# Softmax denominators on a Trainium2 core: which key tiles are added together by DMA, by an elementwise engine and by TensorE

## The chip, the cores and the metric

The kernel runs on one core of one Trainium2 chip. The metric is the device time of one execution in microseconds (us), and lower is better. The kernel before takes 4543.79 us, the median of 3 runs (4541.69 to 4547.17).

The engines are called by the profile's names: PE is TensorE (matmul; PEld is its weight load), DVE is VectorE, ACT is ScalarE, POOL is GpSimd and SP is SyncE, which here only issues DMAs. A name ending in q is an engine's sequencer.

## The reference

The program runs the same two-layer stack twice: an attention layer A and a routed feed-forward layer B, each with a residual. The change touches only the attention of A, which runs twice. Cut to that:

```python
qkv = (x @ wqkv).reshape(B, S, 3, H, Dh).transpose(2, 0, 3, 1, 4)   # S = 2048, H = 32 heads, Dh = 32
q, k, v = qkv[0], qkv[1], qkv[2]
scores = jnp.einsum("bhqd,bhkd->bhqk", q, k) * Dh ** -0.5
p = _softmax(scores, axis=-1)
o = jnp.einsum("bhqk,bhkd->bhqd", p, v)
return o.transpose(0, 2, 1, 3).reshape(B, S, D) @ wo
```

A softmax needs, for every head and query, the sum of the exponentials over all 2048 keys. The kernel leaves the product with v unnormalised and divides by that sum later, so the sums are a piece of work of their own. The change is about how these sums are made.

## The kernel before, in words

**Units and steps.** The attention of a layer is cut into NU = 32 units. A unit is a group of 4 heads with 512 queries. Each unit walks over NT = 16 key tiles of 128 keys, one tile in one step, so a layer has NS = 512 steps. Step s belongs to unit u = s // 16 and key tile kt = s % 16.

**What a step does.** The order of the instructions on every engine is the order in which the Python code emits them. In an ordinary step the loop at L1148 emits: `pre_mm` (matmuls L706 with their row maxima, DVE L714, for the queries of a unit 25 steps ahead), two half steps (`half_step`: scores by PE at L721 into a `pre` PSUM tile, then the exponential by ACT at L1112, two heads at a time), `pre_mm` again, then `pv_step(s - 1)` (PE L1043, the product of the tile before with v), and last `rest_of_step(s)`. The exponentials of a step fill one tile `P[s]`, 128 keys by 4 heads by 512 queries, float32, 1 MB. In the code below P1 means the tile of key tile 1 of its unit.

**Buffers for P.** `P` has PB = 9 buffers. A new tile takes a buffer in the order in which the program gave them back. A buffer is given back by the last instruction that uses its tile, and the exponential that fills it anew waits until this instruction is done.

**The sums.** The 16 tiles of a unit are added up over the keys in three ways:

- A *merge* (`merge`, L1056) is a DMA issued by POOL that adds one P tile to another in place: `merge(u, a, b)` makes P[a] += P[b]. It must wait until PE has read P[a] for the product with v.
- An *add* (`acc_add`, L1053) is one elementwise instruction over 128 x 2048 numbers that adds a P tile to the accumulator `acc` of the unit. It runs on POOL, or on DVE where its last argument is true. The first add of a unit takes two P tiles.
- A *direct* tile goes into the final sum on PE as it is. `sum_mm` (L1063) multiplies a matrix of ones with each direct tile and with `acc`, four matmuls (one for each head) for each of them, into one PSUM tile `st`. ACT copies the result to `sm` (L1073), and SP stores it.

**The order of this work.** `unit_events(left)` lists, for a unit that has `left` units after it, at which step each of these is emitted: (step, "mid" or "end" of `rest_of_step`, priority, what, arguments). A step of 16 or more lies in the next unit. `emit` collects what is due at a step from the unit before and from this one, sorts it and issues it. `EVENTS` holds three lists: for the last unit (`left` 0, all adds on DVE), for the last but one (`left` 1) and for all others. POOL works its list strictly in order, so an instruction that waits holds up all behind it.

**Before**, an ordinary unit has 5 merges (P0+=P1, P6+=P7, P8+=P9, P10+=P11, P12+=P13, emitted at steps 2, 8, 11, 13, 15), 8 adds on POOL (P2 and P3 first, then P0, P5, P4, P6, P8, P10, P12), and the direct tiles 14 and 15. The sum is emitted at step 22, which is step 6 of the next unit. In the last unit but one the adds from step 9 on are on DVE.

**The maxima on SP's queue.** The row maxima of the next unit are put together by DVE in step 6 (`nm_combine`) and step 7 (`nm_row`). SP writes them to DRAM (`nmx<-nmr`, four DMAs) and reads them back into a row of the query tile (`q<-nmx`, two DMAs). The scores of the next unit need them. All of SP's DMAs stand in one queue in the order of the code: the four stores of a sum (`sd<-sm`), then these, and one load of queries, keys or values in each step (`loads`).

**The end of a layer.** `pre_mm` runs 25 steps ahead, so from step 487 there is none. From step 488 (`threes`, L1146) three steps are emitted together, and a third score tile takes the PSUM of two `st` tiles. In step 487 there is no `pv_step`.

Of the kernel before, what the change touches and what calls it, by code (L numbers as in the profile page):

```python
# [19 lines left out]
NT = S // 128  # L20
# [3 lines left out]
NU = NG * QC  # L24
# [9 lines left out]
PB = 9  # L34


MERGED = ((2, 0), (8, 6), (11, 8), (13, 10), (15, 12))
ADDED = ((5, 3), (6, 0), (9, 5), (12, 4), (14, 6), (15, 8), (16, 10), (20, 12))
FIRST = 2
DIRECT = (14, 15)  # L40
LAST_DIRECT = (13, 14, 15)


SLOT_ROWS = (64, 33)
SUM_AT = 22

KEYS_AT = {(2, 14 + 3 * i): slice(i * 512, i * 512 + 512) for i in range(3)}
KEYS_AT[3, 3] = slice(3 * 512, S)

ON_DVE = 9


def unit_events(left):

    if left == 0:
        return [(k + 1, "mid", 1, "add", (k, 0 if k == 1 else None, True)) for k in range(1, NT) if k not in LAST_DIRECT]
    ev = [(at, "end", 0, "merge", (k, k + 1)) for at, k in MERGED]
    ev += [(at, "end", 1, "add", (k, FIRST if at == ADDED[0][0] else None, left == 1 and at >= ON_DVE)) for at, k in ADDED]  # L60
    return ev + [(SUM_AT, "mid", 5, "sum", ())]


EVENTS = [unit_events(i) for i in range(3)]


@with_exitstack
def tile_kernel(ctx, tc, x, wqkv, wo, w_r, w_gate, w_up, w_down, out):
# [29 lines left out]
    def ps_st():  # L98
        return banks["now"][1].tile([128, 512], F32, name="st", bufs=1 if banks["wide"] else 3)

    def ps_pre():
        return psum.tile([128, 1024], F32, name="pre", bufs=2)

    def ps_pv():
        return psum.tile([128, 512], F32, name="pv")
# [544 lines left out]
    def layer(n, src, dst, prev=None, following=None):  # L650
# [93 lines left out]
        with ExitStack() as pst:  # L744
# [209 lines left out]
            for k, (c, wb, i) in enumerate(steps):  # L954
# [26 lines left out]
                at = b - (1, 8)[c == 0]  # L981
# [31 lines left out]
        with sbuf(f"at{n}", bufs=2) as aw:  # L1013
            KS[1] = aw.tile([128, 2, 2, S], F32R, name="ks1", bufs=1)
            P, PV, ACC = {}, {}, {}
# [41 lines left out]

            def sum_mm(u):
                p = ps_st()
                parts = [P[u * NT + k] for k in (DIRECT if u < NU - 1 else LAST_DIRECT)] + [ACC.pop(u).rearrange("p (h c) -> p h c", h=4)]  # L1060
                for i, a in enumerate(parts):
                    for h in range(4):
                        pe.matmul(p[32 * h:32 * h + 32, :], ones32, a[:, h, :], start=(i == 0),  # L1063
                                  stop=(i == len(parts) - 1), tile_position=(0, 32 * h))
                return p
# [12 lines left out]
            def sum_out(u):  # L1078
                store_sum(u, sum_mm(u), aw.tile([128, 512], F32, name="sm", bufs=1))
# [13 lines left out]
            def emit(s, where):  # L1093
                u, kt = divmod(s, NT)
                todo = []
                for back in (1, 0):
                    v = u - back
                    if 0 <= v < NU:
                        todo += [(kt + NT * back, pri, fn, args, v) for (k, pos, pri, fn, args) in EVENTS[min(NU - 1 - v, 2)]
                                 if k == kt + NT * back and pos == where]  # L1100
                for k, _, fn, args, v in sorted(todo, key=lambda e: (-e[0], e[1])):
                    fns[fn](v, *args)

            for i in range(4):
# [11 lines left out]
            def rest_of_step(s):  # L1116
                u, kt = divmod(s, NT)
                pr = pre_rows[s + LEAD] if s + LEAD < NS else None
                emit(s, "mid")
                if pr and pr[1] == 15:  # L1120
                    nm_combine(pr[0])
                if (s + LEAD) % NT == 0 and NT <= s + LEAD - NT < NS:
                    nm_row((s + LEAD) // NT - 1)
                emit(s, "end")
                if s == NS + 1:
                    shared["sum"] = sum_mm(NU - 1)
                if s == NS - 20:
                    shared["first"] = aw.tile([128, 512], F32, name="sm", bufs=1)[:, 0:256]
                    sum_load(shared["first"], 0)
                if s == NS - 17:  # L1130
                    recip(shared["first"], 0)
                if s < NS and kt == 0:
                    queue_loads(u)
                    if u == NU - QC:
                        loads.extend((load_wo, a) for a in range(KD))
                if s == (NU - QC) * NT + 1:
                    right.close()
                    shared["wor"] = ExitStack()
                    wop = shared["wor"].enter_context(sbuf(f"wor{n}", side="right"))
                    shared["WOR"] = wop.tile([128, KD, D], F32, name="wor", bufs=1)  # L1140
                if loads:
                    f, *args = loads.pop(0)
                    f(*args)
# [42 lines left out]
        if True:  # L1186
# [81 lines left out]
            for t in range(NT - 2 if n else NT):  # L1268
                oh, ol = OT.pop(t)
                p = ps_pre()  # L1270
# [60 lines left out]
        if n:  # L1331

            parts = ffn.first_rows(rcols)
            waste = ps_pre()
            p = [[waste[:, h] for h in halves], [ps_st(), ps_pv()]]
            (ah, al), (bh, bl) = (OT.pop(t) for t in (NT - 2, NT - 1))
            both = range(2)
            todo = [(i, x, wol, a, both) for i, x in ((0, ah), (1, bh)) for a in range(KD)]
# [99 lines left out]
```

## Time and profile before

| what | us |
|---|---|
| median of 3 runs | 4543.79 |
| lowest and highest run | 4541.69, 4547.17 |
| the profiled execution | 4545.36 |
| its span, first to last instruction | 4543.6 |
| PE busy | 4497.7 (99%) |
| POOL busy | 3169.1 (70%) |
| DVE busy | 3156.8 (69%) |
| ACT busy | 2426.5 (53%) |

The profile shows one execution. It gives the busy time of each engine, the chain of work that ended last, groups of equal instructions with mean durations and with the idle time ahead of them, and a timeline. The attention runs from about 570 to 2030 us and again in the second layer; between the first and the last units it is strictly periodic, so one unit can be read for all. A shape such as 128x2048 is partitions by elements. Each matmul of the code appears as two records in the trace (8192 records on L1043 for 4096 calls). "x8" in a timeline row means 8 such records in a row.

### The profile page before, as it was taken

What the parts mean: (1) busy time and instruction counts of PE and PEld (TensorE: products, weight loads), DVE (VectorE), ACT (ScalarE), POOL (GpSimd) and SP (SyncE); (2) the same over time, 40 slices, a digit from 0 to 9 for tenths busy, and PEclk for the clock granted to TensorE, in tenths of its full rate; (3) what the DMA queues carried; (4) which work ended last, traced back from release to release, by engine and by line L of the source; (5) the groups of instructions that cost most, each with busy time, mean ns of one, the idle gap of its engine ahead of it and who ended that gap; (6) DMA issues with size and microseconds to landing.
All of it is one profiled execution on the core that took longest, in us unless ns stands there. A gap on an engine that the chain in (4) does not pass through costs nothing.

```text
span 4543.6 us, 73545 instructions
## 1 busy us (share of the span) xinstructions
PE 4497.7 (99%) x29241; PEld 2686.0 (59%) x29241; DVE 3156.8 (69%) x4975; ACT 2426.5 (53%) x2574; POOL 3169.1 (70%) x1239
## 2 busy tenths in 40 slices
PE   9999999999999999999999999999999999999998
PEld 7888755555555555548877786554555555555583
DVE  2211588888888888886522225888888888888763
ACT  3322266767676767670222222776767676767600
POOL 4444378989888889835633343898989898889252
PEclk9999999999999999999999999999999999999998
DMA  6757477777777768759698774777768677777598
GB/s 206 209 174 204 135 170 152 174 153 164 162 167 155 173 143 180 169 131 241 183 319 276 253 208 126 168 161 161 170 144 183 148 166 161 167 155 180 145 275 327
DMA packets 329719, 833.62 MB, mean 183 GB/s; under 512 B 43996, under 2 KB 160732, under 8 KB 280206
## 3 DMA queue, kind: packets, MB, share of 16 engines
q1 hardware_dynamic: 275454, 476.43, 35.8%
q0 software_dynamic: 45248, 325.67, 35.4%
q10 hardware_dynamic: 8672, 26.81, 2.3%
q8 instruction: 230, 3.77, 0.3%
q14 instruction: 115, 0.94, 0.1%
HBM read 384.34 MB, written 119.47 MB: 111 GB/s over the span
## 4 chain that ended last, share of the span: by engine, by line
PE 94%; DMA 2%; DVE 2%; issue 1%; POOL 1%; ACT 0%; SPq 0%; ACTq 0%; POOLq 0%; DVEq 0%
PE pv L1043 22%; PE pre L721 21%; PE st L839 17%; PE st L706 16%; PE pre L839 5%; PE pre L1283 5%; PE st L1063 4%; PE pv L549 1%; PE pre L706 1%; PE pv L839 0%; DMA ord<-rd 0%; PE pre L808 0%; DMA wraw<-in_A_wqkv_dram 0%; DVE acc L1053 0%; PE third L721 0%
## 5 line engine op out<-in xcount | busy, mean ns | idle before, releaser
L714 DVE TENSOR_REDUCE nm<-st 128x1 f32<-128x512 f32 x3916 | 2433.6, 684 | 374.7 <-PE st L706 368.8
L1112 ACT ACTIVATE P<-pre 128x1024 f32<-128x1024 f32 x2016 | 1955.2, 1022 | 704.2 <-PE pre L721 515.6
L1053 POOL TENSOR_TENSOR acc<-acc,P 128x2048 f32<-128x2048 f32 x422 | 2038.4, 4830 | 84.3 <-DMA P<-P 74.7
L721 PE MATMUL pre<-q,ks 64*128 64x512 f32 (+1 forms) x8064 | 1117.8, 395 | 1.7 <-ACT P L1112 1.7
L1043 PE MATMUL pv<-P,v 128*32 128x512 f32 x8192 | 1088.4, 605 | 4.5 <-DMA v<-vd 4.5
L706 PEld LDWEIGHTS st<-ks,q 64*128 64x128 f32 x3916 | 546.5, 184 | 906.8 <-DVE nm L714 765.3
L706 PE MATMUL st<-ks,q 64*128 64x512 f32 x3916 | 982.8, 470 | 0.4
L721 PEld LDWEIGHTS pre<-q,ks 64*128 64x128 f32 (+1 forms) x8064 | 765.2, 186 | 162.1 <-ACT P L1112 27.0
L1056 POOL DMA_DIRECT2D P<-P x310 | 294.2, 949 | 279.2 <-PE st L706 184.6
L854 DVE TENSOR_TENSOR lo<-st,hi 128x512 fp32r<-128x512 f32 x128 | 88.4, 691 | 528.0 <-ACT hi L853 507.9
L774 POOL TENSOR_TENSOR ohl<-wraw,ord 128x2048 fp32r<-128x2048 f32 (+1 forms) x54 | 222.5, 4124 | 308.4 <-ACT ord L769 292.7
L774 POOL TENSOR_TENSOR wl<-wraw,wh 128x2048 fp32r<-128x2048 f32 (+1 forms) x54 | 222.6, 4126 | 303.3 <-ACT wh L773 284.4
L853 ACT CAST hi<-st 128x512 fp32r<-128x512 f32 x128 | 75.4, 589 | 490.9 <-PE st L839 488.6
L1043 PEld LDWEIGHTS pv<-P,v 128*32 128x32 f32 x8192 | 163.3, 108 | 265.4 <-issue 258.2
L1053 POOL TENSOR_TENSOR acc<-P 128x2048 f32<-128x2048 f32 x62 | 295.2, 4761 | 11.0 <-ACT P L1112 11.0
L1283 PE MATMUL pre<-woh,ohl 128*128 128x512 f32 x960 | 223.4, 390 | 1.7 <-DVE pre L1316 0.9
L168 POOL TENSOR_TENSOR rs<-mv,eps_c 128x1 f32<-128x1 f32 x64 | 29.2, 456 | 264.7 <-DVE mv L166 264.7
L1283 PEld LDWEIGHTS pre<-woh,ohl 128*128 128x128 f32 x960 | 179.6, 188 | 42.1 <-ACT ohl L1214 2.1
L839 PE MATMUL st<-xh,wh 128*128 128x512 f32 x512 | 201.2, 393 | 0.0
L839 PE MATMUL st<-xh,wl 128*128 128x512 f32 x512 | 199.3, 389 | 0.0
L839 PE MATMUL st<-xl,wh 128*128 128x512 f32 x512 | 199.2, 389 | 0.0
L1214 ACT CAST ohl<-ord 128x1024 fp32r<-128x1024 f32 x32 | 33.6, 1051 | 272.1 <-DVE ord L1205 81.7
(389 smaller groups left out, 4069.0 us busy)
## 6 DMA issues: line engine op xcount, KB each, us to landing
P<-P POOLq DMA_DIRECT2D x310, 1024.0 KB, 8.9
wraw<-in_A_wqkv_dram SPq DMA_DIRECT2D x96, 1024.0 KB
q<-qh SPq DMA_DIRECT2D x256, 128.0 KB
ks<-kh SPq DMA_DIRECT2D x112, 256.0 KB
fw<-in_B_w_down_dram SPq DMA_DIRECT2D x17, 1024.0 KB
vd<-vn SPq DMA_DIRECT2D x32, 512.0 KB
qh<-hi SPq DMA_DIRECT2D x64, 256.0 KB
ql<-lo SPq DMA_DIRECT2D x64, 256.0 KB
```

Source lines behind the costliest of these rows:

```text
L706: pe.matmul(ps[b], Q[u][rows, i, 0, qt * 128:(qt + 1) * 128], KS[(u // QC) % 2][rows, i, 0, j * 512:(j + 1) * 512], start=True, stop=True, ...
L714: dve.tensor_reduce(NM[u][:, j, 2 * i + b:2 * i + b + 1, qt], ps[b], axis=AX.X, op=OP.max, negate=True)
L721: pe.matmul(p[:, b * 512:(b + 1) * 512], KS[(u // QC) % 2][rows, i, slot, kt * 128:(kt + 1) * 128], Q[u][rows, i, slot, :], start=(slot == ...
L774: pool.tensor_tensor(wl[:, sl], raw[:, sl], wh[:, sl].bitcast(F32), op=OP.subtract)
L839: pe.matmul(p, *pair(a, l, r), start=(a == 0 and k == 0), stop=(a == KD - 1 and k == 2))
L854: dve.tensor_tensor(lo, p, hi.bitcast(F32), op=OP.subtract)
L1043: pe.matmul(PV[u][32 * h:32 * h + 32, :], V[g][:, kt, 32 * h:32 * h + 32], P[s][:, h, :], start=(kt == 0), stop=(kt == NT - 1), tile_posit ...
L1053: (dve if on_dve else pool).tensor_tensor(o, a, P[u * NT + k].rearrange("p h c -> p (h c)"), op=OP.add)
L1056: pool.dma_start(P[u * NT + a], P[u * NT + b], accum_op=OP.add)
L1063: pe.matmul(p[32 * h:32 * h + 32, :], ones32, a[:, h, :], start=(i == 0), stop=(i == len(parts) - 1), tile_position=(0, 32 * h))
L1112: act.activation(P[s][:, 2 * i:2 * i + 2, :].rearrange("p h c -> p (h c)"), p, AF.Exp, scale=SCALE)
L1283: pe.matmul(p[:, bl], l[:, a, :], r[a][:, bl], start=(k == 0 and a == 0), stop=(k == 2 and a == KD - 1))
```

## The change

The two lists of steps become `SUMS` (ordinary units) and `BEHIND_SUMS` (the last unit but one). Ordinary units get six merges instead of five. One of them adds a tile to its predecessor, as all did before (P4+=P5); the other five add a tile to its successor (P2+=P1, P8+=P7, P10+=P9, P13+=P12, P15+=P14). Adds on POOL remain eight. Tile 15 alone is direct, and it then holds tile 14 too. The last unit but one gets three merges instead of five, ten adds on DVE instead of six, and one direct tile. The last unit is as before. The sum of a unit is emitted one step later (23 instead of 22). `emit` sorts by priority first and by age second, where it was the other way round; a step ending in .5 has the priority of 0.5, behind a whole one of the same step.

```diff
-MERGED = ((2, 0), (8, 6), (11, 8), (13, 10), (15, 12))
-ADDED = ((5, 3), (6, 0), (9, 5), (12, 4), (14, 6), (15, 8), (16, 10), (20, 12))
-FIRST = 2
-DIRECT = (14, 15)
+SUMS = (
+    (3, "merge", 2, 1), (5, "merge", 4, 5), (6, "add", 0, 3), (7, "add", 6), (9, "merge", 8, 7), (10, "add", 2), (11, "merge", 10, 9),
+    (11.5, "add", 4), (12, "add", 11), (14, "merge", 13, 12), (14.5, "add", 8), (16, "merge", 15, 14), (17, "add", 10), (19.5, "add", 13))
+DIRECT = (15,)
+
+BEHIND_SUMS = (
+    (3, "merge", 2, 1), (5, "merge", 4, 5), (6, "add", 0, 3), (7, "vadd", 6), (8, "vadd", 2), (9.5, "vadd", 9), (10, "merge", 8, 7), (11, "vadd", 4),
+    (11.5, "vadd", 10), (12, "vadd", 11), (13, "vadd", 12), (14, "vadd", 8), (15, "vadd", 13), (16, "vadd", 14))
+BEHIND_DIRECT = (15,)
 LAST_DIRECT = (13, 14, 15)
...
-SUM_AT = 22
+SUM_AT = 23
...
-ON_DVE = 9
...
-    ev = [(at, "end", 0, "merge", (k, k + 1)) for at, k in MERGED]
-    ev += [(at, "end", 1, "add", (k, FIRST if at == ADDED[0][0] else None, left == 1 and at >= ON_DVE)) for at, k in ADDED]
+    ev = []
+    for at, what, k, *other in (SUMS, BEHIND_SUMS)[left == 1]:
+        args = (k, *other) if what == "merge" else (k, *(other or [None]), what == "vadd")
+        ev.append((int(at), "end", at % 1, "merge" if what == "merge" else "add", args))
     return ev + [(SUM_AT, "mid", 5, "sum", ())]
...
-                parts = [P[u * NT + k] for k in (DIRECT if u < NU - 1 else LAST_DIRECT)] + [ACC.pop(u).rearrange("p (h c) -> p h c", h=4)]
+                parts = [P[u * NT + k] for k in (LAST_DIRECT, BEHIND_DIRECT, DIRECT)[min(NU - 1 - u, 2)]] + [ACC.pop(u).rearrange("p (h c) -> p h c", h=4)]
...
-                for k, _, fn, args, v in sorted(todo, key=lambda e: (-e[0], e[1])):
+                for k, _, fn, args, v in sorted(todo, key=lambda e: (e[1], -e[0])):
```

In the order of POOL's queue an ordinary unit now reads: P2+=P1, (add P13 of the unit before), P4+=P5, add P0 and P3, add P6, P8+=P7, add P2, P10+=P9, add P4, add P11, P13+=P12, add P8, P15+=P14, add P10.

## The prediction

> **What bounds the kernel now.** I read the page first, then one attention unit in windows and in the timeline, engine by engine.
>
> ```profile
> PE 4497.7 (99%) x29241; PEld 2686.0 (59%) x29241; DVE 3156.8 (69%) x4975; ACT 2426.5 (53%) x2574; POOL 3169.1 (70%) x1239
> PE 94%; DMA 2%; DVE 2%; issue 1%; POOL 1%; ACT 0%; SPq 0%; ACTq 0%; POOLq 0%; DVEq 0%
> ...
> 1119.92:1165.72 45.80, 45.80 (x348) 23.17 (x344) 40.14 (x67) 32.12 (x35) 41.06 (x14) 1.00 0.72 153
> 1165.72:1211.52 45.80, 45.80 (x348) 23.18 (x344) 40.13 (x67) 32.09 (x35) 40.98 (x14) 1.00 0.79 175
> ```
>
> The chain that ended last is 94% PE. The windows are two units, cut at the period of the sums below: PE is busy for all 45.80 us of each, so a unit is bound by PE's own instructions. POOL is busy 41 of these, which looks like 5 us to spare, but its time counts in another way: a late add or merge keeps a P buffer, the exponential waits, then PE. The last two columns are the DMA engines' share and GB/s.
>
> ```profile
> 958.37 0.59 ACT L1073 COPY sm<-st 128x512 f32<-128x512 f32 x1 [2.40 <-PE st L1063]
> 1004.17 0.59 ACT L1073 COPY sm<-st 128x512 f32<-128x512 f32 x1 [2.40 <-PE st L1063]
> ...
> 1136.16 0.50 PE L706 MATMUL st<-ks,q 64*128 64x512 f32 x2
> ...
> 1138.74 1.90 PE L1063 MATMUL st<-P,ones 128*32 128x512 f32 x16
> 1140.46 1.04 PE L1063 MATMUL st<-acc,ones 128*32 128x512 f32 x8
> 1141.43 0.50 PE L706 MATMUL st<-ks,q 64*128 64x512 f32 x2
> ...
> 1144.13 0.50 PE L706 MATMUL st<-ks,q 64*128 64x512 f32 x2
> ```
>
> Two sums are 45.80 apart. A plain step is 1144.13 - 1141.43 = 2.70 us. The step with the sum took 1141.43 - 1136.16 = 5.27, so the sum of three tiles costs 2.57. Its two direct tiles run from 1138.74 to 1140.46: 0.86 each.
>
> **The change part by part.** *One direct tile less.* Each layer has 31 units with one direct tile fewer, 62 in all: 62 x 0.86 = 53.3 us of PE (0.85 to 0.87 each: 52.7 to 53.9). The new unit is 44.95 us. All of this is on the path, provided nothing else becomes late.
>
> *The sixth merge, on POOL.*
>
> ```profile
> 1144.78 0.88 POOL L1056 DMA_DIRECT2D P<-P  x1 [2.70 <-PE st L706]
> 1145.39 4.88 POOL L1053 TENSOR_TENSOR acc<-acc,P 128x2048 f32<-128x2048 f32 x1
> 1150.18 0.93 POOL L1056 DMA_DIRECT2D P<-P  x1
> ...
> 1161.00 1.01 POOL L1056 DMA_DIRECT2D P<-P  x1
> 1161.62 5.00 POOL L1053 TENSOR_TENSOR acc<-acc,P 128x2048 f32<-128x2048 f32 x1
> 1167.21 4.59 POOL L1053 TENSOR_TENSOR acc<-acc,P 128x2048 f32<-128x2048 f32 x1 [0.59 <-DMA P<-P]
> ...
> 1175.39 4.57 POOL L1053 TENSOR_TENSOR acc<-acc,P 128x2048 f32<-128x2048 f32 x1 [2.72 <-DMA P<-P]
> 1179.92 4.58 POOL L1053 TENSOR_TENSOR acc<-P 128x2048 f32<-128x2048 f32 x1
> 1184.58 4.57 POOL L1053 TENSOR_TENSOR acc<-acc,P 128x2048 f32<-128x2048 f32 x1
> ```
>
> A merge with the add behind it occupies POOL for 1150.18 - 1144.78 = 5.40 us, a plain add for 4.6 (1179.92 to 1184.58). Five pairs and three adds are 40.8 us; the new six and two are 41.6, of 44.95. There remain 3.3 us a unit, if the waits fit. For that a timetable is needed.
>
> ```profile
> 1006.73 0.50 PE L706 MATMUL st<-ks,q 64*128 64x512 f32 x2
> 1007.07 1.11 PE L721 MATMUL pre<-q,ks 64*128 64x512 f32 x8
> ...
> 1007.80 1.94 ACT L1112 ACTIVATE P<-pre 128x1024 f32<-128x1024 f32 x2 [0.78 <-PE pre L721]
> ...
> 1008.44 1.06 PE L1043 MATMUL pv<-P,v 128*32 128x512 f32 x8
> ```
>
> In a step the exponential runs from 1.07 to 3.01 us after the step begins, and the product of the previous tile ends at 2.77. I count from the start of a new unit: step 7 begins at 18.9, step 8, behind a sum of now 1.71, at 23.3, the next unit at 44.95. A merge into Pk goes out some 0.35 us after Pk's product, that is at the start of step k+2 plus 0.4. POOL's queue then runs: P2+=P1 at 11.2; add P13 of the unit before, to 16.65; P4+=P5 at 16.65; adds P0+P3 and P6, to 26.65; P8+=P7 at 29.15, after 2.5 idle; add P2; P10+=P9 at 34.6; adds P4, P11, to 44.6; P13+=P12 at 44.6; add P8; P15+=P14 at 50.0; add P10, to 55.4; and the next P2+=P1 at 56.15. It closes with 3.3 us idle. Buffers that an add gives back (by the order of the changed program) are asked for later: P13's, free at 16.65, by the exponential of step 7 at 20.0; that is the tightest. The others have 4 us or more. The sum wants P13 and P15 at 21.6.
>
> Buffers that a merge's source gives back wait for the landing of the DMA. The tightest are P12's, asked for in step 4 at 44.95 + 11.9 = 56.8, and P14's, in step 6 at 62.2. Both leave 12.2 us from issue to landing. About 0.5 more costs PE nothing: a second half of scores starts 0.5 us after its `pre` tile is normally free. All else has 13 us or more.
>
> ```profile
> L1056 POOL DMA_DIRECT2D P<-P x310: 850/918/1703, 577.8 to 4232.8; - x155
> DMA to landing us min/median/max: 6.9/8.9/14.6
> ...
> q0 software_dynamic: 641, 4.60, 50.7%
> q1 hardware_dynamic: 1398, 2.37, 21.0%
> ...
> 1135.00:1140.00 5.00, 5.00 (x42) 2.07 (x44) 4.22 (x8) 3.41 (x4) 4.22 (x2) 1.00 0.05 10
> 1140.00:1145.00 5.00, 5.00 (x44) 2.40 (x38) 2.94 (x6) 2.53 (x3) 2.30 (x2) 1.00 0.01 1
> 1150.00:1155.00 5.00, 5.00 (x42) 2.42 (x38) 4.71 (x8) 3.69 (x4) 5.00 (x3) 1.00 1.05 212
> 1160.00:1165.00 5.00, 5.00 (x40) 2.83 (x40) 4.57 (x9) 3.50 (x4) 5.00 (x3) 1.00 1.02 241
> ```
>
> Landings go from 6.9 to 14.6. In the first unit the merges' queue q0 took 50.7% of 45.80 = 23.2 us for 4.60 MB, 5.3 us for a merge. At a share of 0.72 to 0.79 a unit needs 33 to 36 us of the DMA engines; one merge more makes 38 to 41.5, of 44.95. It still fits, and there was room: the share was 0.05 and 0.01 from 1135 to 1145. The long landings of before are the last merges of four that go out 5.4 us apart (1144.78 to 1161.00) while key loads run: the one of 1161.00 landed at 1175.39, as the add waiting for it shows, after 14.4. The new merges go out 5.4, 10, 5.4, 6.2, 5.4 and 12.5 apart, so the backlog is shorter. I take 9 to 12: no stall, with 2 us in all for strays.
>
> The Trainium skill (DMA: Bandwidth & Descriptors, "Anatomy of one DMA — SWDGE (gpsimd) path") fits such a DMA by 2.0 us plus its bytes over 436 GB/s. As an estimate by that page a merge would land after 4.4 us, no buffer would be near late, and the strays would be nothing; this trace's shortest landing, 6.9, is above it, and the trace decides.
>
> *The sum one step later* moves SP's queue.
>
> ```profile
> 1142.18 2.44 SPq L96 DMA_DIRECT2D sd<-sm  x4
> ...
> 1145.21 3.41 SPq L96 DMA_DIRECT2D nmx<-nmr  x4
> 1154.48 1.65 SPq L96 DMA_DIRECT2D q<-nmx  x2
> ```
>
> The stores `sd<-sm` start 0.75 us after the sum's end, and the maxima stand behind them. Before, that was 0.75 after step 7 began (1141.43); now it is 2.70 + 1.71 + 0.75 = 5.16, so 4.4 later, in a unit stretch that grew by 1.7. The last of `q<-nmx` is issued 9.6 us ahead of the next unit in the window (1156.13 against 1165.72) and would be 6.9 ahead. Its landing has no row. The nearest one, the write `nmx<-nmr`, issued by 1148.62, had landed when 1154.48 began, at most 5.9. I take 5.9: it is in time, by 1 us, and costs nothing. The upper end is a merge's 8.9 (rival B).
>
> *The ends of the layers.*
>
> ```profile
> DVE acc L1053 <- DMA P<-P: 14.5, 3, 9.6
> ...
> PE st L1063 <- DVE acc L1053: 1.1, 1, 1.1
> ...
> 1967.74 0.74 PE L721 MATMUL pre<-q,ks 64*128 64x512 f32 x4 [0.69 <-ACT P L1112]
> ...
> 1995.11 28.27 DVE L1053 TENSOR_TENSOR acc<-acc,P 128x2048 f32<-128x2048 f32 x12
> ```
>
> DVE gets four adds more, each 28.27 / 12 = 2.36 us, 9.4 us, and loses two of the merges it sat idle for, 14.5 us in all. Its adds also begin at step 7 instead of 9, so the end moves by nothing or gains. PE's waits of 1.1 and 0.69 may go, so I take 1 us gained a layer (bounds: 9.4 lost, 1.8 gained). The sum: 53.3 + 2 - 2 = 53 us. The profiled execution (4545.36, 1.6 above the median) would give 4492, the median 4543.8 - 53 = 4491; I say 4490.
>
> **The rivals.** *A, DMA backlog in the loaded units.* Key loads run in 14 units of a layer. If P13's or P15's merge there lands after 13.6 us, between the 12.7 allowed and the longest 14.6, PE loses 0.9 in 28 units, 25 us: 4516. For it speaks the share of 1.02 beside the loads; against it the spacing. At 14.6 it would be 53 and the gain gone. The Trainium skill (DMA: Bandwidth & Descriptors, "Issuing engines are not separate DMA queues") has the rule against the change: SP's and POOL's transfers share the same 16 engines and interleave; by that rule the sixth merge lengthens the loads and the loads lengthen it, and the shares above 1 agree.
>
> *B, slower: the maxima come late.* Place: the first scores of a unit wait for `q<-nmx`. If it lands only after a merge's median 8.9, it is 8.9 - 6.9 - 0.6 = 1.4 us late, 62 times, 87 us: 4578. It costs from 7.5 on and makes the kernel slower from 8.4 on. Against it: with a lead of 9.6 PE shows no such wait.
>
> *C, POOL becomes the bound and the saving turns into PE idle.*
>
> ```profile
> L1053 POOL TENSOR_TENSOR acc<-acc,P x422: 4565/4891/5387, 588.8 to 4209.6; 128x2048 f32<-128x2048 f32 x141
> ```
>
> With adds 0.5 us longer, near the longest 5.39, POOL's 41.6 become 45.7, the old period: 4544. Against it, the median 4.89 is the paired add counted above.
>
> **How the numbers follow.** Forecast 0.72 (4490, own range 4483 to 4500), A 0.14 (4516), B 0.08 (4578), C 0.06 (4544). The range of 4483 to 4530 holds the forecast and most of A, and leaves out B, C and A's far end, below 0.2. A difference under 0.2%, 9 us, can't be told from none. Faster is forecast and A, 0.86; same is C, 0.06; slower is B, 0.08.
>
> **What would show it.** Right: sums 44.9 to 45.0 apart; 8 records of `st<-P,ones` less for a unit; PE without idle time; landings mostly under 12.2; POOL idle some 2.5 us ahead of P8+=P7. Wrong: the exponential waiting for a DMA `P<-P` in steps 4 or 6 (A), PE waiting for `q<-nmx` at a unit's start (B), POOL without idle time (C). A stall of 0.86 us in every unit would undo it all.

## The result, and the profile after

| | before | after |
|---|---|---|
| median of the runs, us | 4543.79 (5 runs, 4541.69 to 4547.17) | 4524.05 (5 runs, 4523.86 to 4528.42) |
| span of the profiled execution | 4543.6 | 4522.2 |
| time of a unit in the middle of a layer | 45.80 | 44.93 |

The ratio is 0.9956, with a 95% interval of 0.9945 to 0.9967. The changed kernel is faster by 19.7 us, where 53 were forecast. The time lies inside the range given, but far from the forecast. The medians here and below are of the fast runs; one run of e3, 10643.9 us, was slow and is not in them.

Nearly all units do what was forecast. The copy `o` (ACT, out of PSUM after the last product of a unit) marks the end of each. These rows are from ACT's timeline of the changed kernel; columns are start, length, what:

```profile
1024.11 0.59 ACT L1071 COPY o<-pv 128x512 f32<-128x512 f32 x1
1069.04 0.60 ACT L1071 COPY o<-pv 128x512 f32<-128x512 f32 x1
...
1835.05 0.59 ACT L1071 COPY o<-pv 128x512 f32<-128x512 f32 x1
1881.22 0.60 ACT L1071 COPY o<-pv 128x512 f32<-128x512 f32 x1
1940.69 0.60 ACT L1071 COPY o<-pv 128x512 f32<-128x512 f32 x1
1981.87 0.61 ACT L1071 COPY o<-pv 128x512 f32<-128x512 f32 x1
```

and these from the kernel before, at the end of the layer:

```profile
1855.67 0.59 ACT L1068 COPY o<-pv 128x512 f32<-128x512 f32 x1
1901.45 0.59 ACT L1068 COPY o<-pv 128x512 f32<-128x512 f32 x1
1947.25 0.59 ACT L1068 COPY o<-pv 128x512 f32<-128x512 f32 x1
1990.24 0.60 ACT L1068 COPY o<-pv 128x512 f32<-128x512 f32 x1
```

The differences between these starts are the times of the units. In the middle 1069.04 - 1024.11 = 44.93 us: the direct tile is gone, 0.87 us. At the end stand 46.17, 59.47 and 41.18 where before stood 45.78, 45.80 and 42.99. One interval, from the third last unit into the last but one, is 14.5 us longer than its neighbours. The second layer has 58.79 there. These two places hold 28 us of the 33 that are missing. Another 4.2 and 2.9 us lie in the 28 intervals ahead of it in the two layers, against 2 us that the forecast had allowed for strays: most are 44.93, some 45.1 to 46.2.

Here is the long interval in the view of waits (stretch 1890 to 1915), then in PE's timeline, then cut into three windows (columns: stretch, its length, busy time of PE, PEld, DVE, ACT and POOL, granted clock as a share of full speed, DMA share, GB/s):

```profile
PE st L709 <- DMA q<-qh: 11.5, 1, 11.5
...
1896.18 1.07 PE L1046 MATMUL pv<-P,v 128*32 128x512 f32 x8
1908.76 1.10 PE L709 MATMUL st<-ks,q 64*128 64x512 f32 x2 [11.51 <-DMA q<-qh]
1909.32 2.24 PE L724 MATMUL pre<-q,ks 64*128 64x512 f32 x8
...
1896.20:1908.76 12.56, 1.05 (x10) 0.17 (x9) 1.56 (x4) 1.94 (x2) 8.92 (x2) 0.70 0.96 220
1908.76:1915.56 6.80, 6.80 (x32) 3.32 (x36) 2.69 (x5) 1.94 (x2) 0.00 (x0) 0.54 0.01 4
1915.56:1920.00 4.44, 4.44 (x38) 2.40 (x31) 3.12 (x6) 2.61 (x4) 0.00 (x0) 1.00 0.01 2
```

PE waits 11.5 us for queries. It is the first `pre_mm` for the last unit, whose queries are loaded at the start of the third last unit. After the wait PE works for 6.80 us at a granted clock of 0.54: the eight score records take 2.24 us instead of 1.10. 6.80 x (1 - 0.54) = 3.1 us more, and 11.5 + 3.1 is the 14.5. The Trainium skill (TensorE: Matmul & The Clock Gate, "What's actually happening") has an idle array gated to half its clock until some 3.4 us of sustained work; the trace agrees with the half clock, but 6.80 us at a mean of 0.54 are some 6.2 us of work at half clock, nearly twice that time.

Why the queries are late is seen in SP's queue. After:

```profile
1865.64 6.71 SPq L99 DMA_DIRECT2D wor<-in_A_wo_dram  x7
...
1882.32 4.27 SPq L99 DMA_DIRECT2D q<-qh  x4
1890.41 6.47 SPq L99 DMA_DIRECT2D q<-ql  x2
```

and before:

```profile
1889.66 7.47 SPq L96 DMA_DIRECT2D wor<-in_A_wo_dram  x7
...
1902.55 6.02 SPq L96 DMA_DIRECT2D q<-qh  x4
1910.50 5.55 SPq L96 DMA_DIRECT2D q<-ql  x2
```

Seven of the eight 512 KB loads of the output weights wo go out here, ahead of the last queries; the eighth went out earlier in the fourth last unit. Before, the queries were issued until 1916.05, the DMA engines were busy with them until about 1919.8, and PE used them at 1920.03 without a wait, so this was nearly late already. After, they were issued until 1896.88, PE was ready for them at 1897.25, and they landed 11.5 us later. The loads of wo also hold back the issue itself: between the two `q<-ql` SP stood for nearly 6 us until one of them had landed. Neither load is touched by the diff.

### The profile page after: what moved, and what is told of

The parts are those of the page before. It is cut to its first block, busy times and chain, and to the rows that moved or that the text cites. A ratio compares the mean times of both kernels' runs of the same rounds, so it can differ in the third digit from the quotient of the medians.

```text
span 4522.2 us, 72803 instructions
## 1 busy us (share of the span) xinstructions
PE 4453.7 (98%) x28745; PEld 2669.7 (59%) x28745; DVE 3172.6 (70%) x4983; ACT 2425.3 (54%) x2574; POOL 3213.2 (71%) x1293
## 4 chain that ended last, share of the span: by engine, by line
PE 88%; DMA 6%; DVE 2%; POOL 1%; issue 1%; ACT 1%; SPq 0%; POOLq 0%; DVEq 0%; ACTq 0%
PE pv L1046 20%; PE pre L724 19%; PE st L842 17%; PE st L709 15%; PE pre L1286 6%; PE pre L842 6%; DMA P<-P 3%; PE st L1066 2%; DMA q<-qh 1%; DVE acc L1056 1%; PE pv L552 1%; POOL acc L1056 1%; PE pre L709 1%; PE pv L842 1%; PE pre L811 0%
## 5 line engine op out<-in xcount | busy, mean ns | idle before, releaser
L1059 POOL DMA_DIRECT2D P<-P x366 | 346.7, 947 | 287.1 <-PE st L709 231.2
L1056 POOL TENSOR_TENSOR acc<-P 128x2048 f32<-128x2048 f32 x62 | 307.0, 4952 | 0.0
L1286 PEld LDWEIGHTS pre<-woh,ohl 128*128 128x128 f32 x960 | 180.9, 189 | 45.1 <-ACT ohl L1217 3.5
```

What stands on the lines that cost most here:

```text
L1056: (dve if on_dve else pool).tensor_tensor(o, a, P[u * NT + k].rearrange("p h c -> p (h c)"), op=OP.add)
L1059: pool.dma_start(P[u * NT + a], P[u * NT + b], accum_op=OP.add)
L1286: pe.matmul(p[:, bl], l[:, a, :], r[a][:, bl], start=(k == 0 and a == 0), stop=(k == 2 and a == KD - 1))
```

## The experiments

The kernel before ran beside them with medians of 4545.4 (e1 to e4), 4547.0 (e5 to e8) and 4546.4 us (e9 to e11), so ratios are given too.

**e1: the loads of wo two units later.**

```diff
-                    if u == NU - QC:
+                    if u == NU - 2:
                         loads.extend((load_wo, a) for a in range(KD))
```

> The changed kernel with the eight loads of wo (4 MB) queued from the first step of the last unit but one instead of from the fourth last unit. Theory W (the loads of wo and the merges, now six, share the DMA engines, so the queries of the last unit land 11.5 us late in the third last unit, and PE then runs some 7 us at half clock): the interval of 59.47 us there goes back to 44.95, 2 x 14.5 us less, and the two small waits one unit earlier, 1.2 us each, go too: 4493 (4489 to 4499). Rival A (late landings of the merges, spread over all units): still 4524. Rival T (the new list of the last unit but one costs the time): still 4524.

Measured: 4501.54 us, ratio 0.9903 (0.9887 to 0.9920). The long interval is 44.93 in both layers. So the wait hangs on the loads of wo, and rivals A and T, which had 4524, are out as its cause. The expected time was missed by 8 us; the loads now disturb the place they were moved to: the interval of the last but one unit rises from 41.2 to 46.5. ACT's row and PE's, then the clock:

```profile
1948.00 1.94 ACT L1115 ACTIVATE P<-pre 128x1024 f32<-128x1024 f32 x2 [2.74 <-DMA P<-P]
...
1949.08 0.74 PE L724 MATMUL pre<-q,ks 64*128 64x512 f32 x4 [1.87 <-ACT P L1115]
...
1945.00:1949.08 4.08, 2.21 (x21) 0.80 (x18) 3.03 (x2) 1.34 (x3) 0.07 (x1) 1.00 1.04 256
1949.08:1956.00 6.92, 6.74 (x30) 2.26 (x32) 5.32 (x3) 4.53 (x5) 0.00 (x0) 0.56 0.89 263
```

A merge lands late beside the loads, an exponential waits 2.74 us for its buffer, PE waits 1.87, and the clock falls to 0.56.

**e2: the same move in the kernel before.**

> The kernel before with the same move of the loads of wo. Theory W: there the queries were in time, PE has no wait for them in the trace, so nothing changes: 4544 (4541 to 4547). Rival: the loads of wo cost time in the kernel before too, in some other way, and the move gains 5 us or more: 4539 or less. That would make part of the gain of the first run belong to the move alone.

Measured: 4549.84, ratio 1.0010 (1.0000 to 1.0019). It gains nothing there, so the gain of e1 is not one that the kernel before had to give. The time is 3 us above the expected range; the intervals of both attentions are as before, and in the profiled run the difference lies behind the second attention (308.3 us from its last copy `o` to the end, 304.2 before).

**e3: half of them moved.**

```diff
-                    if u == NU - QC:
-                        loads.extend((load_wo, a) for a in range(KD))
+                    if u in (NU - QC, NU - 2):
+                        loads.extend((load_wo, a) for a in (range(4) if u == NU - QC else range(4, KD)))
```

> The changed kernel with four of the eight loads of wo left in the fourth last unit and four in the last but one. Theory W is a matter of amount: 2.1 MB less ahead of the queries at some 250 GB/s is 8.4 us, so the wait of 11.5 falls to about 3 and the half clock behind it shortens: 4504 (4498 to 4509). Rival: it is the place of the loads in SP's queue, not their bytes, and any load of wo there makes the same wait: 4524.

Measured: 4500.71 (4499.41 to 4504.57), ratio 0.9901 (0.9881 to 0.9921), within the expectation. The long interval is 44.93 and 44.94. Four loads ahead of the queries make no wait, so it is their amount and not that they stand there. The expected rest of 3 us did not show; the four moved loads cost 2 to 4 us at the end instead (44.75 and 43.20).

**e4: one merge less in the fourth last unit, wo left alone.**

```diff
-    for at, what, k, *other in (SUMS, BEHIND_SUMS)[left == 1]:
+    for at, what, k, *other in [e for e in (SUMS, BEHIND_SUMS)[left == 1] if left != 3 or e[:3] != (16, "merge", 15)]:
...
-    return ev + [(SUM_AT, "mid", 5, "sum", ())]
+    return ev + [(SUM_AT - (left == 3), "mid", 5, "sum", ())]
```

`sum_mm` takes tiles 14 and 15 as they are for `left` 3.

> The changed kernel with five merges instead of six in the fourth last unit alone (P15+=P14 left out, tiles 14 and 15 direct, its sum at step 22 again); the loads of wo stay where they are. Theory W (merges and loads share the DMA engines): one merge less, 5.3 us of DMA, shortens the wait of 11.5 us to some 6, for 0.86 us more on PE: 4524 - 2 x 4.4 = 4515 (4509 to 4520). Rival S (the loads of wo and SP's queue alone make the queries late, the merges have no part in it): 4524 + 2 x 0.86 = 4526.

Measured: 4500.73, ratio 0.9903 (0.9886 to 0.9919). Rival S is out: without touching a load, one merge less takes the whole wait away, not half of it as expected. (The experiment also emits this unit's sum at step 22 again. That is not the cause: e9 below does it with six merges, and the wait stays.) The DMA queues show why the amount was misjudged. For the changed kernel from 1882 to 1897, when the queries are being loaded (columns: packets, MB, share of 16 engines):

```profile
q0 software_dynamic: 346, 2.57, 82.4%
q1 hardware_dynamic: 477, 1.20, 21.8%
```

and for e4 from 1880 to 1896:

```profile
q0 software_dynamic: 269, 2.06, 61.8%
q1 hardware_dynamic: 1371, 2.34, 43.5%
```

q0 carries the merges, q1 SP's loads. The engines are full in both. With one merge less q1 moved 2.34 MB instead of 1.20 in a like stretch. Merges that followed each other without a gap left the loads about a fifth of the engines; a gap of one merge doubled what the loads got. The Trainium skill (DMA: Bandwidth & Descriptors, "Issuing engines are not separate DMA queues") says that these transfers interleave on the same engines, and the rows agree.

**e5: four loads of wo behind the last queries.** As e3, with `NU - 3` in the place of `NU - 2`.

> The changed kernel with four loads of wo in the fourth last unit and the other four in the third last, where SP's queue has them behind the last queries of the layer. Theory W: too few bytes stand ahead of the queries, so no wait for them (the first run had 45.4 instead of 59.5 there), and the loads are over before the last unit but one, so its interval stays at 41.2 and does not grow to the 46.5 of the first run: 4497 (4493 to 4502). Rival: four loads in the third last unit hold up its merges, exponentials wait for P buffers, and the time is that of the first run, 4502, or more.

Measured: 4498.06, ratio 0.9892 (0.9876 to 0.9909). No wait for the queries, 41.15 at the end in both layers, as Theory W had it. (The interval of e1 is 44.93, not the 45.4 of the expectation.) The rival is right in one layer: its interval there is 47.87 in the second, 44.98 in the first. There an exponential waited 2.23 us for a merge, PE waited 0.82 and 0.18 us, and then worked 3.42 us at a clock of 0.50 (4130.31 to 4133.73).

**e6: five merges in all ordinary units, new order, sum at 22.** The edit of e4 for every `left` above 1.

> The changed kernel without its sixth merge in all ordinary units: P15+=P14 left out, tiles 14 and 15 direct, sum at step 22. The new order, the new list of the last unit but one and the old place of the loads of wo stay. Theory: the whole steady gain is the direct tile, so units are 45.80 again; the queries of the last unit are in time, so no wait; only the end of the layer keeps its gain of 1.8 us: 4541 (4537 to 4545). Rival: the new order of the merges gains by itself, units under 45.7 and a time below 4530; or it costs by itself, units over 45.9.

Measured: 4539.97, ratio 0.9986 (0.9976 to 0.9996). Units are 45.80 again and the wait is gone. The end is 42.9, as in the kernel before (42.98), so the expected gain of 1.8 us is not there; the next section comes back to it. The 7 us that remain lie outside these intervals: some 2 are PE's waits for the accumulator of the last unit but one, which are gone (1.1 and 0.9 us before), the rest is not placed. So the new order by itself gains nothing in a unit: the gain is the direct tile, and the loss comes with the sixth merge that replaces it.

**e7: the ordinary list in the last but one unit too, on e4.**

```diff
-    for at, what, k, *other in (SUMS, BEHIND_SUMS)[left == 1]:
+    for at, what, k, *other in SUMS:
```

with e4's filter as before.

> The kernel of e4_five_28 with the ordinary list (six merges, all adds on POOL) in the last unit but one too. Theory T0, the prediction's: there a step takes only 2.07 us, POOL needs some 31 us from step 8 on and would end 5 to 7 us behind the sum, so DVE's adds and the fewer merges are worth 5 to 10 us a layer: 4515 (4508 to 4522) against 4501. Rival: POOL and the DMA have room and the special list is worth nothing: 4501 (4498 to 4504).

Measured: 4536.89, ratio 0.9976 (0.9967 to 0.9986). This one changes the computation: where three steps are emitted together, the merges into P10, P13 and P15 come in the program before the products of these tiles with v, so the products read merged tiles and wait for the merges (14.3 us in the first layer between 1940 and 1990; the last interval is 57.8 instead of 41.2). The time is therefore not the price that was asked for, and what the special list is worth against six ordinary merges stays open. What the run shows is that the ordinary list can't stand there.

**e8: the sum at step 22 in all units, on e4.**

```diff
-SUM_AT = 23
+SUM_AT = 22
```

> The kernel of e4_five_28 with the sum at step 22 in every unit. Theory: the step of the sum costs nothing by itself (rival B of the prediction, the row of maxima coming late at 23, is not seen in the trace), and P15's merge lands some 10 us after its issue, 4 us ahead of the sum at 22: 4501 (4498 to 4504), units of 44.95. Rival: at 22 the sum waits for the merge or the last add, units grow by 0.5 us or more: 4530.

Measured: 4491.19, ratio 0.9881 (0.9865 to 0.9898): 9.5 us below e4 where no difference was expected. Its 28 intervals ahead of the one that was long hold 0.1 and 0.3 us over 44.93, those of e4 2.3 and 3.1, of the changed kernel 4.2 and 2.9. The traces thus show 5 of the 9.5 in these intervals. In the profiled runs another 4.5 lie behind the second attention (305.5 us from its last copy `o` to the end in e4, 301.0 in e8), where the two kernels are the same; other runs differ there as much, so this part is not shown to come from the sum. The cause of the 5 us is seen in the waits of the exponential in the ordinary units of the first layer (590 to 1890), for the changed kernel and for e8:

```profile
ACT P L1115 <- DMA P<-P: 9.5, 9, 2.0
```

```profile
ACT P L1115 <- DMA P<-P: 0.9, 2, 0.4
```

and in SP's queue of one unit, again the changed kernel and then e8:

```profile
1119.96 2.65 SPq L99 DMA_DIRECT2D q<-ql  x2
1122.65 1.11 SPq L99 DMA_DIRECT2D ks<-kh  x1
1135.13 2.43 SPq L99 DMA_DIRECT2D sd<-sm  x4
```

```profile
1120.63 2.55 SPq L99 DMA_DIRECT2D q<-ql  x2
1132.93 3.13 SPq L99 DMA_DIRECT2D sd<-sm  x4
1136.11 0.44 SPq L99 DMA_DIRECT2D ks<-kh  x1
```

The load of step 6 stands behind the sum's stores when the sum is emitted in step 6, and ahead of them when it is emitted in step 7. In the changed kernel a key load so gets in beside the merges of the first steps, in e8 it is held until they are over. In the changed kernel 12 of the exponential's 20 waits for a merge stand at step 8, and all 12 in units that load keys or wo.

**e9: the sum at 22 and nothing else.**

> The changed kernel with the sum at step 22 in every unit and nothing else; six merges and the loads of wo as in the change. Theory W2: the sum at 23 lets a key load of step 6 go out ahead of the sum's stores, beside the merges of P15 and P2, whose landing then comes up to 14 us after issue and holds up the exponential of step 8; at 22 this is gone (9 us less, as e8 against e4 showed), but the wait for the last queries, 11.5 us and the half clock behind it, stays, since wo and six merges are still there: 4515 (4510 to 4520). Rival: the sum's place also makes the queries late, and at 22 the wait is gone too: 4490 (4486 to 4496).

Measured: 4515.83, ratio 0.9938 (0.9922 to 0.9955). The small waits go, the long one stays: its interval is 58.09 and 57.47, with PE idle for 10.1 us at the same instruction:

```profile
1906.35 1.26 PE L709 MATMUL st<-ks,q 64*128 64x512 f32 x2 [10.13 <-DMA sd<-sm]
```

The profile puts this wait down to the stores of the sum, that of the second layer (10.3 us) to `q<-qh` as above. The two losses are nearly independent: the long interval is 1.3 to 1.4 us shorter than in the changed kernel, since with the sum in step 6 PE still has the sum's matmuls to do before it needs the queries.

**e10: both losses taken out, six merges everywhere.** e5, with the sum at 22 except in the third last and the last but one unit.

```diff
-    return ev + [(SUM_AT, "mid", 5, "sum", ())]
+    return ev + [(SUM_AT - (left > 2), "mid", 5, "sum", ())]
```

> Six merges everywhere, the sum at 22 except in the third last and the last but one unit (23), four loads of wo in the fourth last and four in the third last unit. If the losses found add up: 4491 of e8, less 0.86 x 2 for its fifth-merge unit, less 0.9 x 2 for the sum of the third last unit in step 487: 4488 (4485 to 4493). Rival: the loads of wo in the third last unit hold up the merges there (47.87 in one of the two layers of e5): 4494.

Measured: 4488.42, ratio 0.9877 (0.9861 to 0.9894), as expected, and below both kernels. The end of its first layer:

```profile
1832.83 0.59 ACT L1071 COPY o<-pv 128x512 f32<-128x512 f32 x1
1877.76 0.59 ACT L1071 COPY o<-pv 128x512 f32<-128x512 f32 x1
1922.69 0.59 ACT L1071 COPY o<-pv 128x512 f32<-128x512 f32 x1
1963.84 0.60 ACT L1071 COPY o<-pv 128x512 f32<-128x512 f32 x1
```

44.93, 44.93 and 41.15: the end of the layer has no wait any more. One interval further ahead is 45.50, all other ordinary units of this layer take 44.93 or 44.94.

**e11: e4 with the sums as in e10.**

> e4_five_28 with the sum at 22 except in the third last and the last but one unit (23); the loads of wo as in the change. Against e8 only the sums of these two units move, of which the first is worth 0.9 us a layer: 4489 (4486 to 4493). Rival: in the third last unit the sum at 23 brings back waits of the exponential, and it is e8's 4491 or more.

Measured: 4495.61, ratio 0.9884 (0.9868 to 0.9901). Its units are clean too but for one of 45.27 (45.80 for the one with five merges, 41.14 at the end), yet the median is above the expectation; the runs lie from 4490 to 4501, and the profiled one, the slowest, lost 4 to 5 us between the two attentions and 6.6 behind the second, against e10. It can't be told from e8.

## Why the prediction was wrong

*The direct tile* was right. 0.87 us a unit against 0.86; e6, which gives it back, has 45.80 again.

*POOL's timetable* was right. The merges of one unit after the change:

```profile
1095.48 0.88 POOL L1059 DMA_DIRECT2D P<-P  x1 [2.29 <-ACT P L1115]
...
1100.90 0.89 POOL L1059 DMA_DIRECT2D P<-P  x1
...
1111.01 0.86 POOL L1059 DMA_DIRECT2D P<-P  x1
...
1116.15 1.16 POOL L1059 DMA_DIRECT2D P<-P  x1
...
1122.51 0.88 POOL L1059 DMA_DIRECT2D P<-P  x1 [0.57 <-PE st L709]
...
1127.91 0.94 POOL L1059 DMA_DIRECT2D P<-P  x1
...
1140.43 0.87 POOL L1059 DMA_DIRECT2D P<-P  x1 [2.29 <-PE st L709]
```

They start 5.4, 10.1, 5.1, 6.4, 5.4 and 12.5 apart (forecast 5.4, 10, 5.4, 6.2, 5.4, 12.5), with 2.3 us idle ahead of P8+=P7 (forecast 2.5). Rival C did not happen. Rival B did not either: no wait of PE names `q<-nmx`. Its lead was sized wrong, without harm: here the last `q<-nmx` was issued at 1141.65, some 14 us ahead of the next unit, where 6.9 was worked out.

*The step that failed* is "provided nothing else becomes late", as it was filled in: the sixth merge's DMA was weighed against an ordinary unit alone ("It still fits"), and only against the buffers that merges give back. The loads on the other queue were never given a deadline. Of all units the fourth last has the most to load, 4 MB of wo, and before the change the transfer of the queries behind it ended only some 0.2 us before PE used them. In place of "nothing else becomes late" the runs showed waits of 11.5 and 11.9 us for these queries in the two layers, with 3.1 us lost at half clock behind the first; e1 and e3 remove them by moving the loads, e4 by leaving out one merge. Rival A had the mechanism, engines shared by merges and loads, but with the wrong victim: P12's and P14's buffers in steps 4 and 6 of units with key loads, 25 us in all. That part was 7 us, and mostly at step 8, for P1's buffer: the forecast took landings of 9 to 12 us, and those of the first layer went up to 14.5.

*The sum one step later* was costed at nothing, with an eye on the row of maxima. What went ahead of it in SP's queue was not counted: the load of step 6 now goes out before the stores `sd<-sm`, as the rows in the result of e8 show. It costs some 6 us in the traces (7.1 us over 44.93 in the changed kernel, 0.9 in e9). It also made PE ready for the last queries sooner, 16.0 us after the copy `o` at the start of the unit instead of 18.6, since the sum's matmuls no longer stand ahead of their first use.

*The ends of the layers*: 1 us a layer was taken, out of PE's two waits of 1.1 and 0.69, and put down to DVE's list. The intervals show 0.9 (42.99 to 41.18 is 1.8 us with the direct tile's 0.87 in it), but that this comes so near to 1 is luck. Both waits went, which makes nearer 2. The wait of 1.1 lies in the last unit, behind these intervals, and is gone in e6 too, which has the new list. The 0.9 is the other wait, and that one comes back wherever the sum of the third last unit is at 22 (e6, e8, e9). In e8:

```profile
1943.76 0.73 PE L724 MATMUL pre<-q,ks 64*128 64x512 f32 x4 [0.72 <-ACT P L1115]
```

There the interval is 42.05, with the same list. So the sum's new step ended this wait, not the list; here the step that was costed at nothing gained 0.9 us a layer.

## What to carry to other kernels

When work moves from the bounding engine to DMAs, give every other transfer a deadline too, and look for the unit with the most to load, not the usual one: a plan that closes in nearly all units lost half of its gain in two of them. Emitting an instruction one step later also lets what stood behind its DMAs in a queue go ahead of them. A DMA that lands late costs more than its lateness if PE falls to half clock behind it.

## What the runs showed of the hardware that was not expected

The two queues did not share the DMA engines by what each needed: with merges following each other the other queue got 21.8% of the engines, with one merge less 43.5%, and its bytes doubled, so a wait of 11.5 us turned on one transfer of 5.3 us. And short waits of PE were enough for the clock to fall: in e1 one of 1.87 us, in a stretch of 4.08 us where PE was busy for 2.21, was followed by 6.92 us at a mean clock of 0.56, and in e5 waits of 0.82 and 0.18 us were followed by 3.42 us at 0.50. Waits of 0.72 and 0.18 us in e8 were not: the clock stayed at 1.00.
